# Attention output of a fused attention and feed-forward kernel: transposed by crossbar DMA from SBUF instead of by PE and a PSUM copy

## The chip, the cores and the metric

The kernel runs on one core of one Trainium2 chip. The metric is the device time of one execution in microseconds (us). The four executions of the kernel before agree within 0.3%.

Names used below: PE is the engine for matrix multiplies (PEld its weight loads), DVE the vector engine, ACT the engine for functions such as exp; SP and gpsimd (POOL in the profiles) issue DMAs, that is, transfers. SBUF is the memory on the core, PSUM the one that matmuls write to.

## The reference

```python
# q, k, v: (8, 8, 576, 64) f32 = batch, heads, tokens, head size; bias_table: (32, 8)
scores = q @ k.T / 8 + bias[bucket(|i - j|)]          # T5-like relative bias
attn   = softmax(scores)
a      = attn @ v                                     # (8, 8, 576, 64)
x      = a.transpose(0, 2, 1, 3).reshape(4608, 512)   # one row per token, 8 heads side by side
h      = x @ w_in                                     # w_in: (512, 2048)
out    = maximum(0.01 * h, h) @ w_out                 # w_out: (2048, 512), out (4608, 512) f32
```

## The kernel before

The work is a list of 32 items: 8 batches, 4 pairs of heads each. For every item the kernel computes scores, exponentials, and attention times v; the result `opair` has tokens on partitions. The feed-forward part needs x with tokens as columns, so each `opair` is transposed into one of four tiles `xT[p]` (128 channels of a head pair x 4608 tokens). Pieces of feed-forward work (`moe(1)`) are mixed into the attention items, so that PE has work while ACT and DVE finish softmax. A token tile T of 512 tokens can start when all four pairs of its last batch are transposed.

```python
    vn = [per.tile([P, NJ, H, D + 1], BF16, name=f"vn{i}") for i in range(NBUF)]   # NBUF = 2
    op_pool   = ctx.enter_context(tc.tile_pool(name="op", bufs=2))
    ps_m_pool = ctx.enter_context(tc.tile_pool(name="ps_m", bufs=3, space=bass.MemoryType.PSUM))
    # ... cut ...
    def av(n, e):                        # attention times v for head e of the pair
        # ... cut: 25 matmuls into ps ...
        nc.vector.reciprocal(rcp, ps[:, :, D : D + 1])
        nc.vector.tensor_tensor(out=opair[:, :, e * D : (e + 1) * D], in0=ps[:, :, 0:D],
                                in1=rcp.to_broadcast([P, NJ + 1, D]), op=ALU.mult)       # L307

    def x_transposes(n):
        b, p = items[n]
        opair = ops_[n]
        ps = ps_m_pool.tile([P, 8 * P], BF16, name="ps_tx", tag="m")
        for ic in range(NJ + 1):                                                         # 5 times
            nc.tensor.transpose(ps[:, ic * P : (ic + 1) * P], in_=opair[:, ic, :], identity=ident)  # L315
        nc.vector.tensor_copy(out=xT[p][:, b * S : (b + 1) * S], in_=ps[:, 0:S])         # L316

    def ffn_in(T):
        # ... cut: 16 groups f ...
            for c in range(n_cc):                                                        # L327
                nc.tensor.matmul(pm, lhsT=w_in_sb[:, c, f * P : (f + 1) * P], rhs=xT[c][:, t0 : t0 + TT],
                                 start=(c == 0), stop=(c == n_cc - 1))
    # ... cut: ffn_out(T), L338, four pieces per 128 tokens ...

    def finished(n):                     # announces that the tokens of a batch are complete
        b, p = items[n]
        if p == n_pairs - 1:
            while made["ready"] < n_tt and (made["ready"] + 1) * TT <= (b + 1) * S:
                made["ready"] += 1

    for n in range(N + 1):
        # ... cut: at pair 1 the loads of q, k and v of the next batch are written ...
        # ... cut: scores and exponentials of item n, av(n - 1, 0), moe pieces ...
        if n > 0:
            av(n - 1, 1)
        if n + 1 < N:
            transpose_k(n + 1)
        moe(1)
        if live:
            ps_a, ps_b = qk_mm(n, 4), qk_mm(n, 5)
            exp_band(n, 4, ps_a)
        moe(1)
        if n > 0:
            x_transposes(n - 1)
            finished(n - 1)
        moe(1)
        if live:
            exp_band(n, 5, ps_b)
        moe(2)
    moe_rest()
```

The softmax here doesn't subtract the row's maximum and nothing guards it: scores larger than these inputs give would overflow.

## Time and profile before

| | before |
|---|---|
| time, median of the first runs | 439.14 us |
| PE in the stretch 100 to 366 us | busy for 265.8 of 266 us, full clock |
| one item there | 11.08 us |
| PE transposes and DVE copies of x | 160 and 32 |

Two rows of the profile page of the kernel before: the span in 40 slices, each digit the busy share of PE in tenths, and then the granted clock of PE in tenths.

```profile
PE   0511888999999999999999999999999999999996
PEclk9999999999999999999999999999999999999999
```

The table of busy time by stretch shows how close to the limit PE is: in 45 us of time it is busy for 45 us.

```profile
core 0: us, PE busy (x) PEld busy (x) DVE busy (x) ACT busy (x) POOL busy (x), PEclk, DMA share, GB/s
145.00:190.00 45.00, 45.00 (x477) 23.30 (x476) 27.77 (x70) 30.13 (x42) 6.97 (x10) 1.00 0.49 66
```

So what is taken from PE there should shorten the kernel, and what makes PE wait there lengthen it; the runs below bear out both (430.83 us with no transposes, 456.46 us with the waits). How much do the transposes cost? The group list (line, engine, operation, count, busy us, mean ns of one) of the kernel before has them as follows.

```profile
L315 PE MATMUL ps_tx<-ident,opair 128*128 128x128 bf16 x160 | 14.5, 222 | 0.0
```

The 222 ns are what one transpose shows by itself, but neighbours overlap. The timeline of PE at a batch boundary (start us, duration, engine, line, operation) shows what the five occupy: from 277.96 to the start of the next group at 278.24, 0.28 us for five.

```profile
277.74 0.38 PE L327 MATMUL pm_4068<-xT_95,w_in_sb 128*128 128x512 bf16 x1
277.96 0.44 PE L315 MATMUL ps_tx<-ident,opair 128*128 128x128 bf16 x5
278.24 1.03 PE L338 MATMUL pm_3928<-w_out_sb,gt 128*128 128x512 bf16 x4
279.10 0.38 PE L327 MATMUL pm_4091<-xT_92,w_in_sb 128*128 128x512 bf16 x1
...
279.75 0.38 PE L327 MATMUL pm_4091<-xT_95,w_in_sb 128*128 128x512 bf16 x1
```

The last line is the first matmul of a new token tile that reads the fourth pair's part of x. The timeline of DVE beside it shows where that part comes from: `opair` is complete at 276.34 (275.85 + 0.49), and the copy out of PSUM ends at 278.90, well ahead of 279.75.

```profile
275.85 0.49 DVE L307 TENSOR_TENSOR opair<-ps_o,rcp 128x320 bf16<-128x320 f32 x1
...
278.44 0.46 DVE L316 COPY xT_95<-ps_tx 128x576 bf16<-128x576 bf16 x1 [0.20 <-PE ps_tx L315]
```

So 3.4 us lie between the end of `opair` and its first use here, 3.1 us once the five transposes themselves are gone.

### The profile page before, as it was taken

What the parts mean: (1) busy time and instruction counts of PE and PEld (TensorE: products, weight loads), DVE (VectorE), ACT (ScalarE), POOL (GpSimd) and SP (SyncE); (2) the same over time, 40 slices, a digit from 0 to 9 for tenths busy, and PEclk for the clock granted to TensorE, in tenths of its full rate; (3) what the DMA queues carried; (4) which work ended last, traced back from release to release, by engine and by line L of the source; (5) the groups of instructions that cost most, each with busy time, mean ns of one, the idle gap of its engine ahead of it and who ended that gap; (6) DMA issues with size and microseconds to landing.
All of it is one profiled execution on the core that took longest, in us unless ns stands there. A gap on an engine that the chain in (4) does not pass through costs nothing.

```text
span 438.2 us, 9059 instructions
## 1 busy us (share of the span) xinstructions
PE 392.3 (90%) x3872; PEld 202.3 (46%) x3872; DVE 229.1 (52%) x581; ACT 247.1 (56%) x338; POOL 60.8 (14%) x84
## 2 busy tenths in 40 slices
PE   0511888999999999999999999999999999999996
PEld 0201554555555555555555555555555454444442
DVE  7331897666666666666666666666666542010111
ACT  1401787887666666666666666666666653333310
POOL 9522103103100310031003100300000000000000
PEclk9999999999999999999999999999999999999999
DMA  8999948708531853184418350900000000101111
GB/s 108 230 225 214 172 71 53 109 4 54 92 65 28 76 83 76 29 76 73 86 27 76 65 94 26 80 25 25 25 25 25 25 25 25 48 29 44 49 48 73
DMA packets 60216, 30.53 MB, mean 70 GB/s; under 512 B 39312, under 2 KB 54800, under 8 KB 60176
## 3 DMA queue, kind: packets, MB, share of 16 engines
q0 software_dynamic: 52960, 18.36, 37.6%
q1 hardware_dynamic: 7216, 11.60, 7.6%
q8 instruction: 30, 0.49, 0.5%
q14 instruction: 10, 0.08, 0.1%
HBM read 37.81 MB, written 10.49 MB: 110 GB/s over the span
## 4 chain that ended last, share of the span: by engine, by line
PE 79%; DVE 7%; DMA 7%; ACT 5%; issue 2%; SPq 0%; DVEq 0%; ACTq 0%
PE ps_o L301 7%; PE ps_s L244 6%; DMA eb_99<-u_rows 5%; PE ps_s L253 2%; DMA u_rows<-ub 2%; PE ps_o L303 2%; ACT at_110 L264 2%; ACT at_111 L264 2%; PE ps_tx L315 2%; PE ps_tq L216 1%; PE ps_tk L227 1%; PE ps_s L250 1%; DVE at_110 L288 1%; DVE opair L307 1%; ACT gt L329 1%
## 5 line engine op out<-in xcount | busy, mean ns | idle before, releaser
L264 ACT ACTIVATE at_111<-ps_s 128x1024 bf16<-128x1024 f32 x64 | 64.7, 1021 | 38.4 <-PE ps_s L244 38.3
L327 PEld LDWEIGHTS <-w_in_sb 128*128 128x128 bf16 x576 | 49.9, 98 | 72.6 <-issue 21.7
L338 PEld LDWEIGHTS <-gt 128*128 128x128 bf16 x576 | 52.6, 98 | 51.4 <-issue 0.4
L264 ACT ACTIVATE at_110<-ps_s 128x1024 bf16<-128x1024 f32 x64 | 64.3, 1021 | 20.6 <-PE ps_s L244 20.4
L288 DVE TENSOR_TENSOR at_110<-at_110,eb 128x512 bf16<-128x512 bf16 (+1 forms) x64 | 32.3, 506 | 53.0 <-ACT at_110 L264 36.8
L288 DVE TENSOR_TENSOR at_111<-at_111,eb 128x512 bf16<-128x512 bf16 (+1 forms) x64 | 32.3, 506 | 44.1 <-ACT at_111 L264 40.0
L244 PE MATMUL ps_s<-qt,kt_109 64*128 64x512 bf16 x128 | 20.8, 396 | 13.7 <-DVE kt_109 L230 13.1
L301 PEld LDWEIGHTS <-at_110 128*128 128x128 bf16 x640 | 28.3, 100 | 10.0 <-DVE opair L307 3.0
L307 DVE TENSOR_TENSOR opair<-ps_o,rcp 128x320 bf16<-128x320 f32 x64 | 31.5, 492 | 2.2
L301 PEld LDWEIGHTS <-at_111 128*128 128x128 bf16 x640 | 27.2, 98 | 9.9 <-DVE opair L307 3.0
L216 PE MATMUL ps_tq<-ident,pr 96*128 96x96 bf16 x192 | 14.2, 212 | 11.5 <-DVE pr L208 11.5
L219 DVE COPY qt<-ps_tq 128x576 bf16<-128x576 bf16 x32 | 23.9, 748 | 0.4 <-PE ps_tq L216 0.4
L244 PE MATMUL ps_s<-qt,kt_108 64*128 64x512 bf16 x128 | 21.6, 403 | 2.3 <-DVE kt_108 L230 1.2
L303 PE MATMUL ps_o<-v_0_106,at_0_112 128*128 128x65 bf16 x80 | 13.7, 200 | 8.9 <-DVE at_0_112 L288 8.8
L303 PEld LDWEIGHTS <-at_0_112 128*128 128x128 bf16 x160 | 15.9, 99 | 9.2 <-DVE at_0_112 L288 9.2
L306 DVE RECIPROCAL rcp<-ps_o 128x5 f32<-128x5 f32 x64 | 12.2, 191 | 11.4 <-PE ps_o L303 11.4
L244 PEld LDWEIGHTS <-kt_109 64*128 64x128 bf16 x128 | 4.2, 94 | 28.1 <-issue 13.8
L301 PE MATMUL ps_o<-vn_104,at_110 128*128 128x65 bf16 x320 | 15.8, 200 | 0.9 <-DVE opair L307 0.8
L123 POOL DMA_DIRECT2D vn_105<-in_v_dram x16 | 14.1, 888 | 15.5 <-PE ps_o L303 7.6
L301 PE MATMUL ps_o<-vn_104,at_111 128*128 128x65 bf16 x320 | 14.5, 194 | 1.7 <-DVE opair L307 1.7
L216 PEld LDWEIGHTS <-pr 96*128 96x128 bf16 x192 | 10.0, 101 | 12.5 <-DVE pr L208 12.4
L303 PEld LDWEIGHTS <-at_1_113 128*128 128x128 bf16 x160 | 15.6, 97 | 0.2 <-DVE at_1_113 L288 0.2
(867 smaller groups left out, 819.1 us busy)
## 6 DMA issues: line engine op xcount, KB each, us to landing
out_dram<-y SPq DMA_DIRECT2D x36, 256.0 KB, 2.0
qn_101<-in_q_dram POOLq DMA_DIRECT2D x4, 576.0 KB, 6.2
kn_103<-in_k_dram POOLq DMA_DIRECT2D x4, 576.0 KB, 8.3
w_in_sb<-in_moe_w_in_dram POOLq DMA_DIRECT2D x4, 512.0 KB, 18.5
w_out_sb<-in_moe_w_out_dram POOLq DMA_DIRECT2D x4, 512.0 KB, 23.0
vn_105<-in_v_dram POOLq DMA_DIRECT2D x16, 128.0 KB, 5.1
qn_100<-in_q_dram POOLq DMA_DIRECT2D x3, 576.0 KB, 6.0
kn_102<-in_k_dram POOLq DMA_DIRECT2D x3, 576.0 KB, 8.8
```

Of the source, the lines that this page charges most:

```text
L123: nc.gpsimd.dma_start(out=vn[i][:, c, h0:h1, 0:D], in_=v[b, h0:h1, c * P : (c + 1) * P, :].rearrange("h s d -> s h d"),)
L216: nc.tensor.transpose(ps[:, c * RQ : (c + 1) * RQ], in_=qs[0:RQ, c, :], identity=ident[0:RQ, 0:RQ])
L219: nc.vector.tensor_copy(out=qt.rearrange("p (r c) -> p r c", c=NC), in_=ps[:, 0:S].rearrange("p (c r) -> p r c", c=NC))
L244: nc.tensor.matmul(ps[:, e, :], lhsT=kt[r, u * P : (u + 1) * P], rhs=qt[r, 0:512], start=True, stop=True)
L264: nc.scalar.activation(at[:, :, u, 0:512], ps, AF.Exp, scale=scale)
L288: nc.vector.tensor_tensor(out=o, in0=o, in1=m, op=ALU.mult)
L301: nc.tensor.matmul(ps[:, ic, :], lhsT=at[:, o : o + P], rhs=vn[i][:, c, 2 * p + e, :], start=(c == 0), stop=False)
L303: nc.tensor.matmul(ps[:, ic, :], lhsT=at4[:, ic * P : (ic + 1) * P], rhs=v4[i][:, p, e, :], start=False, stop=True)
L306: nc.vector.reciprocal(rcp, ps[:, :, D : D + 1])
L307: nc.vector.tensor_tensor(out=opair[:, :, e * D : (e + 1) * D], in0=ps[:, :, 0:D], in1=rcp.to_broadcast([P, NJ + 1, D]), op=ALU.mult)
L327: nc.tensor.matmul(pm, lhsT=w_in_sb[:, c, f * P : (f + 1) * P], rhs=xT[c][:, t0 : t0 + TT], start=(c == 0), stop=(c == n_cc - 1))
L338: nc.tensor.matmul(pm, lhsT=gt[:, f, ts * P : (ts + 1) * P], rhs=w_out_sb[:, f, :], start=(f == 0), stop=(f == n_fc - 1))
```

## The change

The intent is to take the transposes off PE, the copies off DVE and the tile off PSUM, and let one DMA per item do the work: a crossbar transpose, which transposes the data while it moves them. The DMA writes 640 columns for 576 tokens (five blocks of 128), so `xT` grows by 64 columns; the surplus is overwritten by the next batch.

```diff
-    xT = [per.tile([P, NT], BF16, name=f"xT{p}") for p in range(n_pairs)]
+    xT = [per.tile([P, NT + P - SL], BF16, name=f"xT{p}") for p in range(n_pairs)]
@@ x_transposes
         b, p = items[n]
-        opair = ops_[n]
-        ps = ps_m_pool.tile([P, 8 * P], BF16, name="ps_tx", tag="m")
-        for ic in range(NJ + 1):
-            nc.tensor.transpose(ps[:, ic * P : (ic + 1) * P], in_=opair[:, ic, :], identity=ident)
-        nc.vector.tensor_copy(out=xT[p][:, b * S : (b + 1) * S], in_=ps[:, 0:S])
+        w = (NJ + 1) * P
+        nc.sync.dma_start_transpose(
+            out=xT[p][:, b * S : b * S + w].rearrange("p (i t) -> p i t", t=P),
+            in_=ops_[n].rearrange("p i d -> p (i d)"),
+        )
```

## The prediction

> **What bounds the kernel.** From 100 to 420 us PE is the limit: the table of busy time by stage gives PE 45.0 us of every 45.0 there, at full clock, with DVE near 28 and ACT near 30. One item (a batch and head pair) takes 11.08 us. From 55 to 68 us DVE is busy 12.4 of 13.0, and the chain of waits runs through DVE and ACT. The end (366 to 438 us) is feed-forward work alone.
>
> **What the change removes.** Per item five PE transposes and one DVE copy of 128x576 (458 ns). The group list charges the transposes 222 ns each, but that is latency: in the timeline the next matmul starts 0.28 us after the first transpose. About 24 items in the PE-bound stretch give 6.7 us. The copy is worth something only in the first eight items, where DVE and ACT bind: perhaps 2.5 us. Gain about 9 us.
>
> **What it adds.** 32 crossbar transposes of 160 KB on the SP queue, each behind its opair. Most are needed much later. But a new token tile's first feed-forward matmul follows the fourth pair of each batch almost at once: the instruction order shows exactly eight waits of PE on the last pair's DMA, at items 4, 8, ..., 32. From the end of opair to the matmul that needs it the timeline of before leaves, with the transposes taken out, about 3.1 us in the five middle ones (276.3 to 279.5) and 2.3 us in the last (363.0 to 365.3). In the first two the matmul came 2.3 us after opair. PE runs in order, so a later landing is pure loss. With landing time L after opair the loss is about 8L - 22.6 us (L over 3.1); L = 3.9 eats the whole gain.
>
> **L.** [...] 256 KB on SP landed in 2.0 us. I expect more here. The queue table gives 50 ns per packet on the software queue (37.6% of 16 engines for 52,960 packets); if a transpose moves 256-byte rows, its 640 rows on 16 engines are an estimate of 2 us by themselves. And at the first six batch boundaries four loads of v (128 KB each, landing in 4 to 5 us) are issued just when the fourth pair's attention matmuls free the v buffer (99.46 us against opair's end at 100.06), so they share the engines with the transpose. I take L near 4.5 us: loss 13 to 14 us.
>
> **Prediction: 444 us**, 8 in 10 between 431 and 468. Faster by over 2%: 0.09; within 2%: 0.48; slower by over 2%: 0.43.
>
> **What the profile would show.** Right: items near 10.8 us apart in the PE-bound stretch except at batch boundaries; PE idle eight times, 1 to 3 us each, at a new tile's first feed-forward matmul on the fourth pair's part of xT, released by a DMA; transposes landing in 4 to 5 us, slower at the first six boundaries than at the last two; no wait on other items' transposes. Wrong: no such idles and about 430 us (L under 3), or waits away from the boundaries.
>
> **What would make it wrong.** L itself: at 2.5 us the result is about 430, at 6 us about 455[...].

With L = 4.5 us, 8L - 22.6 is 13.4 us of loss, and 439.2 - 9 + 13.4 = 443.6, put down as 444 us. The 4.5 us stand as my estimate, from the 2.0 us of a plain store, the 2 us put on the packets and the loads of v beside them.

## More of the kernel before

The kernel asks the framework to keep PE, ACT and DVE in program order; the SP and gpsimd queues, which issue DMAs, are ordered by the framework's scheduler.

Only the first batch boundary has a wait before the change: 1.15 us at 68.19 us for the copy.

## The result, and the profile after

| | before | after |
|---|---|---|
| median (range) | 439.24 us (439.12 to 440.5) | 456.46 us (453.19 to 457.43) |
| ratio, 95% interval | | 1.0372 (1.0314 to 1.043) |
| one item in the PE-bound stretch | 11.08 us | 10.80 us |
| mean granted clock of PE | 1.0 | 0.985 in the profiled run, 0.977 to 0.98 in the others |

A ratio here is the mean time of one kernel's fast runs over that of the other's of the same rounds, so it is not quite the ratio of the medians. The output is correct. The kernel is slower, though each ordinary item is faster.

The same two rows of the page, now of the changed kernel: PE has holes, and the clock is not full everywhere.

```profile
PE   0412757996999899979999899989999999999996
PEclk9999996998999999998999999999999999999999
```

The view of the transposing line in the changed kernel gives how often and how long each was being issued on the SP queue (min, median, max in ns), who waited for them, and how long from issue to landing.

```profile
L313 SPq DMA_TRANSPOSE xT_95<-opair x8: 1200/1206/1422, 64.9 to 376.2; - x8
...
who waited for it (us, times):
  PE pm_742 L327: 4.8, 1
  PE pm_1319 L327: 3.4, 1
  PE pm_2633 L327: 2.7, 1
  PE pm_3947 L327: 2.0, 1
  PE pm_3290 L327: 1.9, 1
  PE pm_1976 L327: 1.9, 1
  PE pm_5172 L327: 0.2, 1
...
DMA to landing us min/median/max: 2.6/2.9/9.4
```

Every waiter is the first group of a new token tile. Together they are 16.9 us of PE time (the rounded lines above added up). The 9.4 us landing belongs to an early item for which nobody waits. The chain that ended last, in order of time (start, us, what), holds the same landings:

```profile
64.88 5.43 DMA xT_95<-opair
...
104.38 5.29 DMA xT_95<-opair
...
151.41 5.12 DMA xT_95<-opair
...
196.68 5.95 DMA xT_95<-opair
...
244.37 5.13 DMA xT_95<-opair
...
289.66 5.24 DMA xT_95<-opair
...
376.21 2.58 DMA xT_95<-opair
```

The first six boundaries have 5.1 to 6.0 us from issue to landing. The seventh is missing from the chain: nobody waited, and it landed in 2.6 us, as did the eighth. One boundary in the timeline, first PE, then the gpsimd queue:

```profile
154.30 0.38 PE L327 MATMUL pm_1976<-xT_94,w_in_sb 128*128 128x512 bf16 x1
156.57 0.38 PE L327 MATMUL pm_1976<-xT_95,w_in_sb 128*128 128x512 bf16 x1 [1.89 <-DMA xT_95<-opair]
...
150.78 3.53 POOL L123 DMA_DIRECT2D vn_104<-in_v_dram  x4 [2.65 <-PE ps_o L303]
```

The bracket says that PE stood idle for 1.89 us until the transposing DMA landed. The gpsimd line says that four loads of v began to be issued at 150.78, released by the attention matmuls (L303) that also complete this `opair`; the transpose was issued at 151.41, into the middle of them.

The queue list shows what a transpose is made of. Columns: packets, MB, share of 16 engines; first the kernel before, then the changed one.

```profile
q1 hardware_dynamic: 7216, 11.60, 7.6%
```

```profile
q1 hardware_dynamic: 28720, 16.85, 14.8%
```

That is 21,504 more packets, 672 per transpose. The packet records of the trace have them as 640 of 256 bytes and 32 of 4 bytes, the row size that the prediction assumed. The added time of the 16 DMA engines is 14.8% of 16 x 451.4 us less 7.6% of 16 x 438.2 us, about 25 ns per packet.

### The profile page after: what moved, and what is told of

Its sections match the earlier page's. It is cut to its first block, busy times and chain, and to the rows that moved or that the text cites. A ratio compares the mean times of both kernels' runs of the same rounds, so it can differ in the third digit from the quotient of the medians.

```text
span 451.4 us, 8797 instructions
## 1 busy us (share of the span) xinstructions
PE 388.3 (86%) x3712; PEld 194.1 (43%) x3712; DVE 214.3 (47%) x549; ACT 246.6 (55%) x338; POOL 60.7 (13%) x84
## 3 DMA queue, kind: packets, MB, share of 16 engines
q1 hardware_dynamic: 28720, 16.85, 14.8%
## 4 chain that ended last, share of the span: by engine, by line
PE 74%; DMA 14%; DVE 7%; ACT 3%; issue 1%; SPq 0%; DVEq 0%
DMA xT_95<-opair 8%; PE ps_s L244 7%; PE ps_o L301 7%; DMA eb_99<-u_rows 5%; PE ps_o L303 2%; DMA u_rows<-ub 2%; PE ps_s L253 2%; DVE opair L307 2%; PE ps_tq L216 1%; ACT at_110 L264 1%; PE ps_tk L227 1%; PE pm_2639 L338 1%; PE ps_s L250 1%; ACT at_111 L264 1%; PE pm_1325 L338 1%
## 5 line engine op out<-in xcount | busy, mean ns | idle before, releaser
L338 PEld LDWEIGHTS <-gt 128*128 128x128 bf16 x576 | 53.7, 98 | 70.4 <-issue 14.6
L301 PEld LDWEIGHTS <-at_110 128*128 128x128 bf16 x640 | 29.2, 101 | 10.5 <-DVE opair L307 2.6
L244 PE MATMUL ps_s<-qt,kt_109 64*128 64x512 bf16 x128 | 22.6, 426 | 12.6 <-DVE kt_109 L230 11.9
L301 PEld LDWEIGHTS <-at_111 128*128 128x128 bf16 x640 | 27.2, 98 | 9.6 <-DVE opair L307 3.0
L244 PE MATMUL ps_s<-qt,kt_108 64*128 64x512 bf16 x128 | 21.6, 396 | 4.0 <-DVE kt_108 L230 2.3
L303 PE MATMUL ps_o<-v_0_106,at_0_112 128*128 128x65 bf16 x80 | 13.6, 200 | 10.1 <-DVE at_0_112 L288 10.1
L303 PEld LDWEIGHTS <-at_0_112 128*128 128x128 bf16 x160 | 16.1, 101 | 10.2 <-DVE at_0_112 L288 10.2
L303 PEld LDWEIGHTS <-at_1_113 128*128 128x128 bf16 x160 | 15.6, 97 | 0.0
```

Source lines behind the costliest of these rows:

```text
L244: nc.tensor.matmul(ps[:, e, :], lhsT=kt[r, u * P : (u + 1) * P], rhs=qt[r, 0:512], start=True, stop=True)
L301: nc.tensor.matmul(ps[:, ic, :], lhsT=at[:, o : o + P], rhs=vn[i][:, c, 2 * p + e, :], start=(c == 0), stop=False)
L303: nc.tensor.matmul(ps[:, ic, :], lhsT=at4[:, ic * P : (ic + 1) * P], rhs=v4[i][:, p, e, :], start=False, stop=True)
L338: nc.tensor.matmul(pm, lhsT=gt[:, f, ts * P : (ts + 1) * P], rhs=w_out_sb[:, f, :], start=(f == 0), stop=(f == n_fc - 1))
```

## The clock

The table of busy time by stretch of the changed kernel has a new column of interest, PEclk (after the POOL column): 0.72 around the first boundary and 0.83 around the fourth, 1.00 in quiet stretches.

```profile
66.00:78.00 12.00, 7.65 (x69) 3.73 (x69) 4.21 (x12) 4.55 (x6) 2.57 (x4) 0.72 0.97 60
...
157.00:197.00 40.00, 40.00 (x430) 20.25 (x430) 22.62 (x57) 27.85 (x37) 3.09 (x5) 1.00 0.41 71
197.00:207.00 10.00, 7.28 (x41) 2.58 (x41) 3.29 (x9) 3.36 (x5) 3.24 (x4) 0.83 1.26 99
```

The clock records of the trace list three stretches at half clock in the profiled run, each beginning in the last microsecond of a wait or in the one after it:

```
start us   length us   clock
 69.62       6.83       0.5     (after the 4.8 us wait)
110.58       3.41       0.5     (after the 3.4 us wait)
202.74       3.41       0.5     (after the 2.7 us wait)
```

The waits of 1.9 and 2.0 us drew none. Half clock for 13.65 us loses at most 6.8 us of PE work (an upper estimate, as a small part of it lies in the waits themselves). The other three runs, at 0.977 to 0.98, lose at most 9.1 to 10.5 us by the same reckoning (an estimate: 0.02 x 453.9 to 0.023 x 455.7 us); no trace of them was kept.

A mean clock of 0.996 to 1.0, as in most runs below, need not mean any loss: in every profiled run of that kind the only half clock recorded begins after the last matmul.

## The experiments

### No transpose at all: the gain by itself

```diff
     def x_transposes(n):
         b, p = items[n]
-        w = (NJ + 1) * P
-        nc.sync.dma_start_transpose( ... )
+        return
@@ once, before the loop over items
+    for t in xT:
+        nc.vector.memset(t, 0.01)
```

Expected:

> The changed kernel with no transpose of the attention output at all: x^T is filled once with a constant, so the result is wrong on purpose, and no matmul waits for anything but the constant. It measures the gain term alone: what PE transposes and their copies cost the kernel before. If 0.28 us of PE per item and a little of DVE is right: 439.2 - 9 = about 430 us (0.979 of before), clock 1.0, items 10.8 us apart in the PE-bound stretch with no longer gaps at the batch boundaries. If the gain was mis-sized because the transposes really cost their listed 222 ns x 160 of PE time: about 404 us.

Measured: 430.83 us (430.14 to 430.9) against 439.64, ratio 0.9798 (0.9783 to 0.9813), clock 0.998 to 1.0, items 10.8 us apart in the PE-bound stretch with no longer gaps at the batch boundaries. The gain term is 8.8 us, against 9 predicted. About 7.0 us of it come from the 24 items after the first eight (0.29 us each); of the rest, 1.15 us are the wait at the first boundary, which is gone too. The 222 ns reading of a transpose would have meant four times as much.

### Both: crossbar traffic without anyone needing it

```diff
         nc.vector.tensor_copy(out=xT[p][:, b * S : (b + 1) * S], in_=ps[:, 0:S])
+        scr = scr_pool.tile([P, (NJ + 1) * P], BF16, name="scr")                # a pool of four; its line is cut
+        nc.sync.dma_start_transpose( ... scr <- opair, as in the change ... )
```

Expected:

> The kernel before, with the 32 crossbar transposes added beside the PE transposes; they write a scratch buffer that nobody reads. It measures whether crossbar traffic by itself slows anything. If the loss of the changed kernel comes only from PE waiting for the landing: within 0.5% of before (438 to 441 us), and the transposes of the fourth pair still land in about 5 us at the first six boundaries and in under 3 us at the last two. If crossbar traffic disturbs loads or engines by itself: over 443 us.

Measured: 439.77 us, ratio 1.0006 (0.9986 to 1.0025). Thirty-two crossbar transposes beside everything else cost nothing that can be seen. The median landing of all 32 was 3.6 us. In the trace the fourth pairs landed in 5.2 to 6.6 us at the first six boundaries, 2.6 us at the seventh and 4.1 us at the eighth, where under 3 us was expected. So the landing is as long when nobody needs it, and the loss must come from somebody waiting.

### Moving the loads of v: a first attempt that changed nothing

The loads of v for batch b + 1 go out when the last pair of batch b - 1 frees their buffer, which is just at the batch boundary. The edit wrote them later in the program, behind the loads of q and k of the batch after:

```diff
-            elif p == 1 and 0 < b < B - 1:
-                load_qk(b + 1, 0, H)
-                load_v(b + 1, 0, H, False)
+            elif p == 3:
+                if b + 2 < B:
+                    load_qk(b + 2, 0, H)
+                if 0 < b < B - 1:
+                    load_v(b + 1, 0, H, False)
```

Expected, for the changed kernel and then for the kernel before as a control:

> The changed kernel with only the order of the gpsimd loads altered: the loads of v for the next batch go out about two items after the batch boundary, behind the loads of q and k of the batch after it. Theory (the fourth pair's landing is stretched from 2.6 to 5.2 us by the loads of v that are issued at the same moment): xT_95 lands in 2.6 to 3.3 us everywhere, no wait at the five middle boundaries, about 2 us at the first and 1 us at the second, clock at 0.99 to 1.0, time 430 to 435 us (0.98 to 0.99 of before). Rival (the landing takes 5 us there for another reason, such as the queue of output stores, the fourth pair's position or the state of PE): landing stays near 5 us and the time stays at 453 to 457 us.

> Control: the kernel before with the same reordering of the loads. Both theories: no change, 438 to 441 us, since no engine waits for these loads there. If it is faster by over 1%, the gain of the reordered changed kernel is not due to the transposes' landing.

Measured: 457.08 us (ratio 1.0392) and 439.48 us (ratio 0.9998). This decides nothing: the scheduler orders the gpsimd queue itself, and both programs came out with the same order of loads as without the edit. The trace shows the loads of v at the boundaries as before (151.60 us and a landing of 5.29 us at the third). The expectation of the first run was not met because its premise was not. Its use is as a repeat of the changed kernel: it had five half-clock stretches (20.5 us) where the first profile had three (13.65 us), waits of 17.7 us in place of 16.9, and a span of 455.7 in place of 451.4 us. Half of 6.8 us and 0.8 us of waits account for 4.2 of these 4.3 us, so the number of half-clock stretches accounts for most of the difference between these two runs.

### Moving the loads of v, with the queue held in program order

```diff
-    ctx.enter_context(tc.manual_schedule(engines={ET.PE, ET.Activation, ET.DVE}))
+    ctx.enter_context(tc.manual_schedule(engines={ET.PE, ET.Activation, ET.DVE, ET.Pool}))
```

with the edit above. The v of the last batch has no later load of q and k ahead of it, and still goes out at the sixth boundary.

Expected:

> The previous attempt to move the loads of v left the order of the gpsimd queue as it was. Here that queue is kept in program order, so that the loads of v for batches 2 to 6 wait behind the loads of q and k of the batch after and go out about two items after the boundary; the last batch's v (7) has nothing ahead of it and still goes out at the sixth boundary, an inner control. Theory (landing stretched by the loads of v issued at the same moment): xT_95 lands in 2.6 to 3.3 us at the boundaries 1 to 5, 7 and 8 and in about 5 us at the 6th; waits of PE about 2 us at the first, 1 us at the second, 0 at the 3rd to 5th, 2 us at the 6th; time 433 to 438 us (0.985 to 0.997 of before). Rival (the landing takes 5 us at the first six boundaries for another reason): near 5 us at all six, 453 to 457 us.

Measured: 437.31 us (435.82 to 440.36), ratio 0.9958 (0.9917 to 0.9999), clock 0.996 to 0.999. The landings of `xT` in the chain that ended last of this run (names are merged in this trace, start and us as above):

```profile
66.56 2.59 DMA xT<-opair
...
100.91 2.56 DMA xT<-opair
...
273.29 4.26 DMA xT<-opair
...
358.86 2.58 DMA xT<-opair
```

The first two boundaries fell from 5.4 and 5.3 us to 2.6; the third to fifth dropped out of the chain, with items 10.8 us apart across them, and landed in 2.6 us too; the sixth, where the v of the last batch was issued 0.19 us ahead of the transpose (273.10 and 273.29 us), kept 4.26 us (about 5 was expected). The waits of PE were 2.0, 0.7, 1.0 and 0.2 us at the first, second, sixth and eighth boundary, 3.8 us in all; 2 us was expected at the sixth.

The same trace has a second sign. The loads of v now go out with those of q and k beside a second pair's transpose, and it is this one that lands late: 7.5 to 7.9 us at five places where the changed kernel had 2.7 to 4.8. Nobody waits for it. One of them, as issued (ns) and to its landing, where the changed kernel had 3.0 us:

```profile
L313 SPq DMA_TRANSPOSE xT<-opair x1: 1272/1272/1272, 122.0 to 122.0; - x1
DMA to landing us min/median/max: 7.5/7.5/7.5
```

The loads of v are therefore what stretches the landing at the boundaries. The rival, that the fourth pair's landing is slow for a reason of its own, falls.

A control with the same two edits in the kernel before:

> Control for the kernel with the later loads of v: the kernel before with the gpsimd queue in program order and the same later loads. The chain of waits of that run started about 2 us later (its table of the bias landed at 43.6 us instead of 41.8), which I put down to the new order of the first loads and not to the transposes. If so: 440 to 442 us here. If the time is 439.3 or less, the 436 to 440 us of the changed kernel with later loads has a part that is still unexplained.

Measured: 440.2 us, ratio 1.0016 (0.9999 to 1.0033). The later start costs perhaps 0.4 us on the median (440.2 against 439.83), less than I expected from the chain. The profiled run took 435.82 us; against the floor of 430.8 us, its 3.8 us of waits and 0.4 us leave 0.8 us. Its clock explains none of that, for the half clock of this run begins at 433.38 us and its last matmul ends at 430.06. The other three runs, of 437.03 to 440.36 us, have no trace; their extra time stays open.

### The fourth pair back on PE

```diff
     def x_transposes(n):
         b, p = items[n]
+        if p == n_pairs - 1:
+            # the five PE transposes and the DVE copy of the kernel before
+            return
         w = (NJ + 1) * P
```

Expected:

> Part of the change undone: the fourth pair of each batch is transposed on PE with a DVE copy as before, the other three pairs by the crossbar. Theory (only the fourth pair's landing is waited for): no PE wait on a transposing DMA, clock near 1.0, and three quarters of the gain: 439.6 - 0.75 x 8.8 = about 433 us (0.984 to 0.987). If the landings of the other pairs, or the crossbar traffic, cost anything: over 437 us.

Measured: 434.06 us (433.99 to 434.41), ratio 0.9877 (0.9862 to 0.9891), clock 0.998 to 1.0, and no wait of PE for a transposing DMA. The time is 1 us above the number expected and the ratio a hair above its range. Most of that was to be expected: the 8.8 us contain the wait of 1.15 us at the first boundary, which belongs to the fourth pair and stays (1.2 us in this run, for the DVE copy), so three quarters of it, 0.9 us, cannot be gained. The mechanism is as expected. Undoing a quarter of the change takes away all of its loss.

### Filling the waits with idle matmuls

```diff
+    FILL = (24, 16, 9, 9, 9, 9)
@@ ffn_in
         for f in range(n_fc):
+            if f == 0 and T <= 5:
+                pd = ps_m_pool.tile([P, TT], FP32, name="pd", tag="m")
+                for _ in range(FILL[T]):
+                    nc.tensor.matmul(pd, lhsT=w_in_sb[:, 0, 0:P], rhs=w_in_sb[:, 1, 0:TT], start=True, stop=True)
             pm = ps_m_pool.tile([P, TT], FP32, name="pm1", tag="m")
```

Expected:

> The changed kernel with idle matmuls (results thrown away) put in front of the new token tile's first feed-forward group at the first six boundaries: 24, 16, 9, 9, 9, 9 of 512 columns, 0.216 us each at full clock, about as long as the waits were. They only fill the time in which PE would wait. Theory (beside the waits themselves, the PE idle time makes the granted clock drop for several us after some of them): clock 0.995 to 1.0, and time about 446 to 449 us, some 7 to 10 us less than the changed kernel (454 to 457 us). Rival (the lower mean clock costs nothing or has another cause): the clock stays at 0.98 and the time at 453 us or over, since the work added fills the waits exactly or overshoots.

Measured: 450.3 us (449.37 to 452.68), ratio 1.0253, clock 0.996 to 1.0; the profiled run has no half-clock stretch between start and end of its matmuls. One line of the list of waits of this run shows what is left of the waits, 2.0 us in three of them:

```profile
PE pm L332 <- DMA xT<-opair: 2.0, 3, 1.1
```

Work that is thrown away made the kernel 6 us faster, so the half clock after the waits is a cost of its own: at least 6 of the 17 us lost (the filling takes 16.4 us and 2.0 us of waits remain, 1.5 us more than the waits that it replaced). The sum closes too: 430.8 (no transposes) + 76 x 0.216 (idle matmuls) + 2.0 = 449.2 us. The median is 1 us over the range expected.

### Starting a new token tile later

```diff
         if n + 1 < N:
             transpose_k(n + 1)
+        if n > 1:
+            finished(n - 2)
         moe(1)
@@
             x_transposes(n - 1)
-            finished(n - 1)
+            if not live:
+                finished(n - 1)
```

Expected, and then the control, the same edit in the kernel before:

> The changed kernel with a new token tile started about half an item later (the batch's end is announced after the next item's second key transpose), so that PE has other work while the transpose lands; the final boundary is as it was. Same matmuls, other order. Theory (the loss is the wait for the landing at the boundaries and what follows it): no waits at the first seven boundaries, at most 0.3 us at the last, clock near 1.0, time 430 to 434 us. If something else of the crossbar transposes costs the time: over 437 us.

> Control for the deferred start: the kernel before, PE transposes and DVE copies kept, with the same later start of a new token tile. Theory (the deferral alone gains nothing in the kernel before, which waited only 1.2 us at one boundary): 438 to 441 us, so that deferring and crossbar together are what gives 432.5. Rival (the deferral itself is the improvement, by a better order of pieces): 431 to 434 us.

Measured: 432.55 us (432.06 to 432.81), ratio 0.9839 (0.9823 to 0.9856), clock 0.998 to 1.0, and no wait of PE for a transpose. The control: 441.36 us, ratio 1.0046 (1.0025 to 1.0066), just above the range expected, so the later start alone costs about 1.5 us. The same crossbar transposes, with the loads of v still beside them (the fourth pairs land in 5.2 to 6.4 us at the first six boundaries of this run's trace), are worth 1.6% once nobody needs them at once. This version beats both kernels, clear of the noise; it is 1.7 us above the run with no transposes.

## Why the prediction was right or wrong

The direction and most of the mechanism were right, and the measured 456.46 us lies inside the range of 431 to 468; the point of 444 us was 12 us too low. The odds were less good: within 2% had the most (0.48), slower by over 2% had 0.43, and 3.7% slower is what came. Term by term:

| step | predicted | measured |
|---|---|---|
| gain | 9 us | 8.8 us (no transposes at all; 1.15 us of it is the wait before the change) |
| item in the PE-bound stretch | 10.8 us | 10.80 us |
| places of the waits | eight batch boundaries only | boundaries 1 to 6 and 8; 0 at the 7th |
| landing L | near 4.5 us, slower at the first six | 5.1 to 6.0 at the first six, 2.6 at the last two |
| PE waits above those of before | 13 to 14 us | 15.7 us (16.9 less 1.15) |
| granted clock | not considered | at least 6 us of the median by the filled run; at most 6.8 us in the profiled run by its clock records |

- What bounds the kernel: right. PE was the limit, and taking away 0.28 us per item gave 0.28 us per item.
- The eight exposed landings: right in place, though the seventh made nobody wait. Slack decided the size: the first two boundaries, with less work between `opair` and its use, waited 4.8 and 3.4 us, the middle four 1.9 to 2.7 us.
- L: the cause (loads of v released by the same matmuls) was right and is shown by moving them (5.4 and 5.3 us fell to 2.6 at the first two boundaries); the size was too small by 0.6 to 1.5 us at the six boundaries. The trace has 2.6 us for an undisturbed transpose (issued at 376.21), 0.94 us of it from its first to its last data packet (377.38 to 378.32) and 1.64 us before and after them. A plain store of 256 KB on SP landed in 2.0 us in all, with 0.83 us of moving data in it. The 2 us that I put on the transpose's packets was too much: they took these 0.94 us. That 4.5 us came near the mean of the eight landings, 4.7 us, is therefore luck in part: too much for the packets, too little for the loads, and too much at the last two boundaries.
- The step that failed: "a later landing is pure loss", with the loss equal to the wait. A wait of 2.1 us or more could also be followed by 3.4 or 6.8 us at half clock, and the prediction did not look for it. Filling the waits shows that it is a cost apart, of at least 6 us.

The sum for the profiled run: 439.2 - 8.8 + 16.9 + 6.8 = 454.1 us against 453.19 us measured. The waits stand here in full, because the 8.8 us already contain the 1.15 us of before; that the sum is 0.9 us too high fits the 6.8 us being an upper estimate.

What stays open is where in the stretched landing the time goes. In the packet records the disturbed transpose of 151.41 us had its first data packet 1.88 us after issue (1.17 undisturbed, at 376.21), moved data for 1.21 us (0.94), sent its last 4-byte packet 0.68 us after that (0.01), and landed 1.35 us later (0.46). All four parts grow. Whether the loads' number of packets, their writes or their completions do it was not tried.

## What to carry to other kernels

In this kernel the operation moved from a compute engine to a DMA was free only where its result wasn't needed for the whole landing time (2.6 us undisturbed, 5.1 to 6.0 us at the first six boundaries). So list the consumers, find those that come soon after the producer, and measure the slack there, not on average. Look at what the same event releases on other queues, for that may be under way beside the new DMA, as the loads of v were here (5.43 us to landing at the first boundary, 2.59 us with the loads moved). Where PE must wait, count the half clock afterwards too: here 3.4 or 6.8 us of it could follow waits of 2.1 us or more. Two cures worked here: to keep the change and move the first consumer (432.55 us), or to leave only the urgent part on the old path (434.06 us).

## What was measured of the hardware here

- The landing of a crossbar transpose: undisturbed (the one issued at 376.21 us), 160 KB landed in 2.6 us; beside four loads of v on the software queue it took 5.1 to 6.0 us, and 2.6 again once these loads were moved (4.26 us at the boundary where they stayed).
- What the issuing queue pays: each transpose of 128x640 held the SP queue for 1.2 us, against 0.33 us for an output store of 256 KB.
- The rate of single transfers: one undisturbed transpose of 160 KB moved its packets in 0.94 us, 174 GB/s, and one plain store of 256 KB on the same queue of the same run in 0.83 us, 317 GB/s. The rate of a long stream was not measured.
- The clock after waits of PE: waits of 4.8, 3.4 and 2.7 us (first profile) and 2.1, 2.2 and 2.5 us (the repeat) were followed by half clock, while another of 2.1 us was not, nor were those of 1.9 and 2.0 us. The half clock lasted 3.41 or 6.83 us.
- Transposes on PE: each 128x128 bf16 transpose shows 219 ns in the trace (the median), and in a stream of matmuls five of them took 0.28 us, some 56 ns each.
